# Attention and a gated feed-forward on one core: two products of the second layer split once more, with their sums on GpSimd

## The chip, the core and the metric

The kernel runs on one NeuronCore of a Trainium2 chip. Its engines run side by side, each with its own queue of instructions, and wait for one another through semaphores: TensorE (PE, matmuls; its weight loads are listed as PEld), VectorE (DVE), ScalarE (ACT), GpSimd (POOL) and SyncE (SP), which here only issues transfers. TensorE writes into PSUM[...]; VectorE and ScalarE read PSUM[...]. Everything else lives in SBUF, a memory of 128 partitions.

The metric is the device time of one execution in microseconds (us). Comparisons leave disturbed runs out.

## The reference

Linear attention without softmax, a norm per head, and a feed-forward layer with a sigmoid gate:

```python
# q, k, v: (8 batches, 8 heads, 576 positions, 64), float32
kv  = einsum('bhsd,bhse->bhde', k, v)
o   = einsum('bhsd,bhde->bhse', q, kv)
x   = o / sqrt(mean(o * o, axis=-1) + 1e-6) * g_norm       # then (4608 tokens, 512)
h   = sigmoid(x @ w_gate) * (x @ w_val)                    # (4608, 1536)
out = h @ w_out                                            # (4608, 512)
```

The weights come as 8-byte floats and are converted on the chip. All matmuls are in fp32.

## The kernel before

Tokens are worked in nine chunks of 512 (`G`). Chunk 0 is computed with plain matmuls while weights still arrive; chunks 1 to 8 each run a *first layer* (x to h) and a *second layer* (h to out), and both use a scheme of Strassen's kind: a product of two matrices, each cut into 2 x 2 blocks, takes seven block products in place of eight, and sums of blocks before and after. In the first layer some of the seven are split by seven once more. In the second layer, the blocks of h are halves of its tokens and of its 1536 columns (`NFT` = 12 tiles of 128, so `NF2` = 6), and the blocks of w_out are halves of its rows and columns (`DH` = 256). The sums of h are made by VectorE at the end of the first layer, the sums of w_out (`t2w`) once.

```python
P, G, GH = 128, 512, 256                     # GH: half a chunk; h1, h2: its two halves

def sg_tile():                               # gates, and results on their way out
    return sb.tile([P, G], FP32, tag="sg", name="sg", bufs=4)

free = deque([4, 2, 3, 0, 1])                # PSUM banks
def take():
    i = free.popleft()
    return i, bank(i)[:, 0:GH]
def give(i):
    free.append(i)

def slot():                                  # one step of other work, between matmuls
    if fill:
        fill.popleft()()

# sums of h, when one = gv[c, f] and two = gv[c, f + NF2] are done
s12[c, f] = s = hp.tile([P, G], FP32, tag="gv", name="s12")
tt(out=s[:, h1], in0=one[:, h2], in1=two[:, h2], op=ALU.add)
tt(out=s[:, h2], in0=s[:, h1], in1=one[:, h1], op=ALU.subtract)          # L854
tt(out=one[:, h2], in0=one[:, h1], in1=one[:, h2], op=ALU.subtract)
tt(out=s4[c, f], in0=two[:, h1], in1=s[:, h2], op=ALU.subtract)

def second_layer_fast(c):
    b = {(j, n): w2[:, NF2 * (j - 1):NF2 * j, DH * (n - 1):DH * n] for j in (1, 2) for n in (1, 2)}
    d1, d2 = slice(0, DH), slice(DH, DM)
    for g in range(2):
        t1, t2 = slice(P * g, P * g + P), slice(GH + P * g, GH + P * g + P)
        (i_a, pa), (i_b, pb) = (take() for _ in range(2))
        last = (c, g) == (NG - 1, 1)         # here two products are cut into halves of 128 columns
        parts = [slice(0, DH // 2), slice(DH // 2, DH)] if last else [slice(0, DH)]

        def product(ps, hs, ws, new):
            for f in range(NF2):
                nc.tensor.matmul(ps, hs(f), ws[:, f, :], start=(new and f == 0), ...)    # L870
                if f % 3 == 2:
                    slot()

        product(pa, lambda f: gv[c, f][:, t1], b[1, 1], True)
        o2 = sg_tile()
        nc.scalar.copy(out=o2[:, d1], in_=pa)
        product(pb, lambda f: s12[c, f][:, t2], t2w[2], True)
        o1 = sg_tile()
        tt(out=o1[:, d2], in0=pb, in1=o2[:, d1], op=ALU.add)
        product(pa, lambda f: gv[c, f + NF2][:, t1], b[2, 1], False)     # the one product of two added in PSUM
        nc.scalar.copy(out=o1[:, d1], in_=pa)
        if last:
            store(c, g, o1, d1)
        product(pb, lambda f: gv[c, f][:, t2], t2w[3], False)
        tt(out=o2[:, d2], in0=pb, in1=o2[:, d1], op=ALU.add)
        # ... product of s12 (t1) with t2w[1], added to o2[:, d2]
        product(pb, lambda f: gv[c, f + NF2][:, t2], t2w[4], False)
        tt(out=o2[:, d1], in0=pb, in1=o2[:, d1], op=ALU.add)
        store(c, 2 + g, o2)
        # ... product of s4 (t1) with b[2, 2], added to o1[:, d2]
        if not last:
            store(c, g, o1)
        if g == 1:
            load_late(c + 2)                 # keys and values of a later batch
```

Around it, in the order in which they are issued:

```python
def store(c, t, ot, cols=slice(0, DM), queues=(nc.sync,)):
    # ... pieces of n rows that are together in DRAM; for batches from 2 on n is 32, 64 or 96:
    queues[i % len(queues)].dma_start(
        out=rows.rearrange("(r p g i) d -> i r g p d", p=QB, g=JH, i=2)[half, r, c0 // QB:(c0 + n) // QB],
        in_=ot[r0:r0 + n, cols])             # QB = 32: g of 1, 2 or 3, p of 32

def load_late(b):                            # 9 tiles of 128 x 512 that take over tiles of h
    # ... mains[n, name] = hp.tile(..., tag="gv"), filled by nc.sync.dma_start, for k and v

def feed(b):                                 # attention for batch b, as steps for slot():
    # ... turns of q (DVE), kv_mm (PE, L354), copies (ACT), u_mm (PE, L395), squares, roots, norms,
    #     x_turn (DVE, L420) and the transfers that put x into xT

def x_sums(c):                               # the eight sums of x for the next first layer, by VectorE
    # ... four of 128x512 (L691 to L694), four of 128x128 (L701 to L704)

for c in range(1, NG):
    if c + 1 < B:
        steps = feed(c + 1)
        if c == 1:                           # the sums of w_out, in twelve pieces, on VectorE
            i = 4
            while w2_sums:
                steps.insert(i, (DVE, w2_sums.popleft()))
                i += 3
        spread(steps, ...)
    first_layer_fast(c)                      # p1 of each of its six steps: matmuls, then a sg tile
    sums_of(c + 1)                           # x_sums go to the end of the steps
    second_layer_fast(c)
    flush()                                  # what is left of the steps
```

In the first layer the sums of the weights for the next step (`tw`, L720, and `tx`, L713) are made by GpSimd, with `nc.gpsimd.tensor_tensor`.

Of the kernel before, what the change touches and what calls it, by code (L numbers as in the profile page):

```python
# [10 lines left out]
FP32 = mybir.dt.float32  # L11
# [4 lines left out]
ALU = mybir.AluOpType  # L16
# [4 lines left out]
def kernel(  # L21
# [11 lines left out]
    nc = tc.nc  # L33

    B, H, S, HD = q.shape
    T, DM = out.shape
    DF = moe_w_gate.shape[1]
    P = 128
# [22 lines left out]
    NFT = DF // P  # L61
    G = 512
    GH = G // 2
    NG = T // G
# [3 lines left out]
    sb = ctx.enter_context(tc.tile_pool(name="sb", bufs=2))  # L68
# [36 lines left out]
    def load_late(b):  # L105


        if b >= B:
            return
        mains = {}  # L110
        for n in range(NHP):
            for name, src in (("k", k), ("v", v)):
                mains[n, name] = t = hp.tile([P, G], FP32, tag="gv", name="kv")
                nc.sync.dma_start(out=t.rearrange("p (h c) -> p h c", h=2),
                                  in_=src[b, 2 * n:2 * n + 2, 0:S4].rearrange("h (p j) d -> p h (j d)", j=NK4))
        rest = hp.tile([P, G], FP32, tag="gv", name="kv")
        for i, src in enumerate((k, v)):
            for r in range(2):
                nc.sync.dma_start(out=rest[PH * r:PH * r + PH, GH * i:GH * i + GH].rearrange("p (h d) -> p h d", d=HD),
                                  in_=src[b, NHP * r:NHP * r + NHP, S4:S].rearrange("h p d -> p h d"))  # L120
        kv_late[b] = mains, rest
# [213 lines left out]
    def slot():  # L335
        if fill:
            fill.popleft()()
# [122 lines left out]
    def spread(steps, at):  # L460

        n = 0
        for engine, step in steps:
            while engine == DVE and n < 7 * NF2 and n % 7 not in at:
                fill.append(idle)
                n += 1
            fill.append(step)
            n += 1

    def flush():  # L470
        while fill:
            fill.popleft()()

    gv = {}
# [3 lines left out]
        return gv[c, f]  # L478

    def sg_tile():  # L480
        return sb.tile([P, G], FP32, tag="sg", name="sg", bufs=4)

    def store(c, t, ot, cols=slice(0, DM), queues=(nc.sync,)):

        r0 = i = 0
        while r0 < P:
            b, s = divmod(G * c + P * t + r0, S)
            rows = out[S * b:S * b + S, cols]
            if b < 2:
                j, p = divmod(s, NP)  # L490
                n = min(P - r0, NP - p)
                queues[i % len(queues)].dma_start(out=rows.rearrange("(p j) d -> j p d", j=NJ)[j, p:p + n],
                                                  in_=ot[r0:r0 + n, cols])
            else:
                half, c0 = divmod(s, S // 2)
                r, c0 = divmod(c0, XC)
                n = min(P - r0, XC - c0)
                queues[i % len(queues)].dma_start(
                    out=rows.rearrange("(r p g i) d -> i r g p d", p=QB, g=JH, i=2)[half, r, c0 // QB:(c0 + n) // QB],
                    in_=ot[r0:r0 + n, cols])  # L500
            r0 += n
            i += 1
# [7 lines left out]
    def bank(i):  # L510
        return (psum_mm if i < 2 else psum).tile([P, 512], FP32, tag=f"mm{i}", name="mm")
# [3 lines left out]
    def mm0_ps():  # L515
        return bank(next(turns0) % 2)

    def mm_ps():
        return bank((2, 3, 0, 1)[next(turns) % 4])

    def at_ps():
        return psum.tile([P, NQ, 512], FP32, tag="at", name="at")
# [4 lines left out]
# [7 lines that stand above are left out]
    def early(n):  # L534

        shared = []

        def ps(kind):
            if kind == "q":
                return shared[0]  # L540
            t = psum0.tile([P, 2, 512], FP32, tag="kq" if kind == "kv" else f"ux{n % 2}", name="two")
            if kind == "kv":
                shared.append(t)
                return t[:, :, JH * P:]
            return t
        return ps


    class Plain:
# [9 lines left out]
        def gate(self):  # L559
            self.sg = sg_tile()  # L560
            nc.scalar.activation(out=self.sg, in_=self.ps[0], func=AF.Sigmoid)
# [18 lines left out]
    a = [attention(n, early(n)) for n in range(NE)]  # L580
# [19 lines left out]
    for token in order.split():  # L600
        name = token.rstrip("0123456789.")
        n = [int(i) for i in token[len(name):].split(".")]
        f = n[0]
        if name == "b":
            if f not in blks:
                if f == 3:
                    psum_ctx.__exit__(None, None, None)
                    psum = ctx.enter_context(tc.tile_pool(name="psum", bufs=1, space=bass.MemoryType.PSUM))
                    ps = (mm_ps(), mm_ps())
                else:  # L610
                    ps = (mm0_ps() if f else warm, mm0_ps())
# [29 lines left out]
    for f in range(4, NFT):  # L641
        if f == NFT - 1:
            last = at_ps()
# [6 lines left out]
    ps = [mm_ps() for _ in range(G // P)]  # L650
# [22 lines left out]
    NF2 = NFT // 2  # L673
    DH = DM // 2
    h1, h2 = slice(0, GH), slice(GH, G)
    tt = nc.vector.tensor_tensor
    sx, tw, s12, s4 = {}, {}, {}, {}
# [171 lines left out]
    def h_sums(c, f):  # L849
# [5 lines left out]
        tt(out=one[:, h2], in0=one[:, h1], in1=one[:, h2], op=ALU.subtract)  # L855
        tt(out=s4[c, f], in0=two[:, h1], in1=s[:, h2], op=ALU.subtract)

    def second_layer_fast(c):
        b = {(j, n): w2[:, NF2 * (j - 1):NF2 * j, DH * (n - 1):DH * n] for j in (1, 2) for n in (1, 2)}
        d1, d2 = slice(0, DH), slice(DH, DM)  # L860
        for g in range(2):
            t1, t2 = slice(P * g, P * g + P), slice(GH + P * g, GH + P * g + P)
            (i_a, pa), (i_b, pb) = (take() for _ in range(2))

            last = (c, g) == (NG - 1, 1)
            parts = [slice(0, DH // 2), slice(DH // 2, DH)] if last else [slice(0, DH)]

            def product(ps, hs, ws, new):
                for f in range(NF2):
                    nc.tensor.matmul(ps, hs(f), ws[:, f, :], start=(new and f == 0), stop=(f == NF2 - 1),  # L870
                                     skip_group_check=True)
                    if f % 3 == 2:
                        slot()

            product(pa, lambda f: gv[c, f][:, t1], b[1, 1], True)
            o2 = sg_tile()
            nc.scalar.copy(out=o2[:, d1], in_=pa)
            product(pb, lambda f: s12[c, f][:, t2], t2w[2], True)
            o1 = sg_tile()
            tt(out=o1[:, d2], in0=pb, in1=o2[:, d1], op=ALU.add)  # L880
            product(pa, lambda f: gv[c, f + NF2][:, t1], b[2, 1], False)
            nc.scalar.copy(out=o1[:, d1], in_=pa)
            if last:
                store(c, g, o1, d1)
            product(pb, lambda f: gv[c, f][:, t2], t2w[3], False)
            tt(out=o2[:, d2], in0=pb, in1=o2[:, d1], op=ALU.add)
            pcs = []
            for x in parts:
                i_c, pc = take()
                pc = pc[:, 0:x.stop - x.start]  # L890
                pcs.append((i_c, pc))
                product(pc, lambda f: s12[c, f][:, t1], t2w[1][:, :, x], True)
                o2x = o2[:, DH + x.start:DH + x.stop]
                tt(out=o2x, in0=pc, in1=o2x, op=ALU.add)
            product(pb, lambda f: gv[c, f + NF2][:, t2], t2w[4], False)
            tt(out=o2[:, d1], in0=pb, in1=o2[:, d1], op=ALU.add)
            store(c, 2 + g, o2)
            give(i_a)
            give(i_b)
            for (i_c, pc), x in zip(pcs, parts):  # L900
                give(i_c)
                product(pc, lambda f: s4[c, f][:, t1], b[2, 2][:, :, x], False)
                y = slice(DH + x.start, DH + x.stop)
                tt(out=o1[:, y], in0=pc, in1=o1[:, y], op=ALU.add)
                if last:
                    store(c, g, o1, y, (nc.sync, nc.scalar))
            if not last:
                store(c, g, o1)
            if g == 1:
                load_late(c + 2)  # L910

    def sums_of(c):
        if c < NG:
            fill.append(lambda: fill.extendleft(reversed(x_sums(c))))
# [17 lines left out]
    t2w = {i: sums.tile([P, NF2, DH], FP32, name=f"t2w{i}", bufs=1) for i in (2, 3, 4)}  # L932
# [14 lines left out]
# [3 lines that stand above are left out]
            if c == 1:  # L950

                i = 4
                while w2_sums:
                    steps.insert(i, (DVE, w2_sums.popleft()))
                    i += 3
            spread(steps, (1, 2, 3, 4, 5) if c == 1 else (2, 3, 4, 5))
        first_layer_fast(c)
        sums_of(c + 1)
        second_layer_fast(c)
        flush()  # L960
# [30 lines left out]
```

## Time and profile before

| what | us |
|---|---|
| time, median of 3 runs | 1076.38 (1076.11 to 1077.92) |
| span of the profiled execution | 1073.9 |
| TensorE busy | 1062.2 |
| VectorE busy | 712.0 |
| GpSimd busy | 442.1 |
| ScalarE busy | 309.0 |
| one second layer with attention's matmuls in it (chunk 5) | 38.3 |
| one second layer without (chunk 7) | 36.3 |

A line of groups in the profile names the line of the kernel, the engine, the operation, the tiles written and read with their shapes, the count, the busy time in us and the mean of one in ns, and after the second bar the idle time of the engine just before, with what ended most of it. A line of the timeline or of the chain gives start and length in us, counted from the start of the span. Matmuls are pipelined: a record lasts longer than the distance to the next one.

### The profile page before, as it was taken

The numbers are of one execution on the slowest core, as the hardware profiler recorded it, in microseconds if no ns is written. First come the engines' busy times: TensorE is split into PE (matmuls) and PEld (weight loads), VectorE is DVE, ScalarE is ACT, GpSimd is POOL, SyncE is SP. The second block draws the span as 40 slices with busy tenths as digits, with TensorE's granted clock in tenths as the row PEclk, the third lists the DMA queues.
The fourth block names the chain that finished last, engine by engine and source line by source line (L and its number), as shares of the span: only waits on it lengthen the run. The fifth ranks groups of instructions, "written<-read, shape, count | busy, mean of one in ns | idle before, by whom it ended". The sixth has DMA issues, their size and how long they took to land.

```text
span 1073.9 us, 19464 instructions
## 1 busy us (share of the span) xinstructions
PE 1062.2 (99%) x7514; PEld 882.4 (82%) x7514; DVE 712.0 (66%) x1461; ACT 309.0 (29%) x737; POOL 442.1 (41%) x630
## 2 busy tenths in 40 slices
PE   8999999999999999999999999999999999999997
PEld 7544448888888888888888888888888888888886
DVE  4897767894579547863778357945786388628841
ACT  4654323331243113320433134312431122112210
POOL 0000035880367216640666046713663077307800
PEclk9999999999999999999999999999999999999999
DMA  9944710002400141012301140014001200010001
GB/s 259 254 157 157 244 29 22 24 17 60 119 12 13 45 128 36 12 35 62 100 23 34 42 120 13 25 45 137 13 12 27 58 2 1 2 38 1 1 1 40
DMA packets 69115, 64.96 MB, mean 60 GB/s; under 512 B 23712, under 2 KB 63008, under 8 KB 69024
## 3 DMA queue, kind: packets, MB, share of 16 engines
q1 hardware_dynamic: 68768, 63.69, 21.1%
q8 instruction: 60, 0.98, 0.4%
q14 instruction: 31, 0.25, 0.1%
q10 hardware_dynamic: 256, 0.03, 0.1%
HBM read 47.19 MB, written 9.44 MB: 53 GB/s over the span
## 4 chain that ended last, share of the span: by engine, by line
PE 97%; DVE 1%; DMA 1%; SPq 0%; issue 0%; ACT 0%; DVEq 0%
PE mm L728 46%; PE mm L870 27%; PE mm L732 7%; PE mm L556 7%; PE mm L653 4%; PE at L395 2%; PE at L354 1%; PE at L556 1%; DMA q<-in_q_dram 1%; PE two L291 0%; PE two L261 0%; PE mm L634 0%; PE two L318 0%; PE two L272 0%; PE at L360 0%; SPq L97 0%
## 5 line engine op out<-in xcount | busy, mean ns | idle before, releaser
L720 POOL TENSOR_TENSOR tw<-gv 128x256 f32<-128x256 f32 x192 | 156.2, 823 | 232.1 <-DVE w L202 145.0
L728 PE MATMUL mm<-xT,tw 128*128 128x256 f32 x768 | 198.4, 381 | 0.0
L728 PE MATMUL mm<-sx,tw 128*128 128x256 f32 x768 | 197.4, 380 | 0.0
L802 POOL TENSOR_TENSOR sg<-sg 128x256 f32<-128x256 f32 x48 | 35.6, 742 | 341.1 <-ACT sg L801 340.9
L720 POOL TENSOR_TENSOR tw<-gv,tw 128x256 f32<-128x256 f32 x192 | 155.0, 828 | 0.0
L728 PEld LDWEIGHTS mm<-xT,tw 128*128 128x128 f32 x768 | 137.3, 190 | 17.5 <-issue 2.9
L728 PEld LDWEIGHTS mm<-sx,tw 128*128 128x128 f32 x768 | 134.9, 191 | 12.4
L773 DVE TENSOR_TENSOR gv<-gv,sg 128x256 f32<-128x256 f32 x192 | 108.7, 585 | 0.0
L728 PE MATMUL mm<-sx,gv 128*128 128x256 f32 x384 | 91.2, 380 | 0.0
L728 PE MATMUL mm<-xT,gv 128*128 128x256 f32 x384 | 90.8, 379 | 0.0
L870 PE MATMUL mm<-w,gv 128*128 128x256 f32 x384 | 89.1, 381 | 0.7 <-DVE gv L773 0.7
L870 PE MATMUL mm<-t2w,gv 128*128 128x256 f32 x384 | 88.7, 381 | 0.0
L870 PE MATMUL mm<-w,s 128*128 128x256 f32 (+1 forms) x408 | 88.3, 367 | 0.0
L764 ACT ACTIVATE sg<-sg 128x256 f32<-128x256 f32 x96 | 40.0, 416 | 151.0 <-DVE sg L763 150.9
L739 ACT COPY sg<-mm 128x256 f32<-128x256 f32 x96 | 35.8, 373 | 162.7 <-PE mm L728 160.9
L870 PEld LDWEIGHTS mm<-w,gv 128*128 128x128 f32 x384 | 72.5, 190 | 12.2 <-DVE gv L773 2.5
L870 PEld LDWEIGHTS mm<-w,s 128*128 128x128 f32 x408 | 74.1, 190 | 9.4
L728 PEld LDWEIGHTS mm<-xT,gv 128*128 128x128 f32 x384 | 72.9, 190 | 10.4 <-issue 0.5
L728 PEld LDWEIGHTS mm<-sx,gv 128*128 128x128 f32 x384 | 72.5, 190 | 10.0
L870 PEld LDWEIGHTS mm<-t2w,gv 128*128 128x128 f32 x384 | 72.4, 190 | 10.0
L556 PE MATMUL mm<-xT,gv 128*128 128x512 f32 x176 | 77.4, 594 | 0.0
L745 DVE TENSOR_TENSOR gv<-mm,sg 128x256 f32<-128x256 f32 x96 | 37.0, 413 | 41.2 <-PE mm L728 37.8
(120 smaller groups left out, 1548.4 us busy)
## 6 DMA issues: line engine op xcount, KB each, us to landing
q<-in_q_dram SPq DMA_DIRECT2D x24, 288.0 KB
st<-in_moe_w_gate_dram SPq DMA_DIRECT2D x12, 512.0 KB
st<-in_moe_w_val_dram SPq DMA_DIRECT2D x12, 512.0 KB
st<-in_moe_w_out_dram SPq DMA_DIRECT2D x12, 512.0 KB
kv<-in_k_dram SPq DMA_DIRECT2D x24, 256.0 KB
kv<-in_v_dram SPq DMA_DIRECT2D x24, 256.0 KB
out_dram<-sg SPq DMA_DIRECT2D x23, 192.0 KB
xT<-xTs SPq DMA_DIRECT2D x48, 72.0 KB
```

Source lines behind the costliest of these rows:

```text
L395: nc.tensor.matmul(u[HD * e:HD * e + HD, r, o:o + HD], qTs[QB * r:QB * r + QB, (n0 + which) % 2, c:c + PH], kvq[QB * r:QB * r + QB, (n0 + ...
L556: nc.tensor.matmul(self.ps[i], w[("wg", "wv")[i], self.f][:, m, :], xT[self.c][:, m, :], start=(m == 0), stop=(m == NMT - 1), skip_group_c ...
L653: nc.tensor.matmul(ps[t], gv[0, f][:, P * t:P * t + P], w["wo", f], start=(f == 0), stop=(f == NFT - 1), skip_group_check=True)
L720: nc.gpsimd.tensor_tensor(out=tw[f, i], in0=b[in0], in1=b[in1] if isinstance(in1, tuple) else tw[f, in1], op=ALU.subtract)
L728: nc.tensor.matmul(ps, wt[:, m, :], xs[:, m, :], start=(new and m == 0), stop=(m == NK - 1), skip_group_check=True)
L732: nc.tensor.matmul(ps, wt, xs, start=new, stop=True, skip_group_check=True)
L739: nc.scalar.copy(out=d["sg"][:, h2], in_=d["pa"])
L745: tt(out=d["h"][:, h1], in0=d["pb"], in1=d["sg"][:, h2], op=ALU.add)
L764: nc.scalar.activation(out=d["sg"][:, h2], in_=d["sg"][:, h2], func=AF.Sigmoid)
L773: tt(out=d["h"][:, h], in0=d["h"][:, h], in1=d["sg"][:, h], op=ALU.mult)
L802: nc.gpsimd.tensor_tensor(out=g2[:, h1], in0=g2[:, h1], in1=g2[:, h2], op=ALU.add)
L870: nc.tensor.matmul(ps, hs(f), ws[:, f, :], start=(new and f == 0), stop=(f == NF2 - 1), skip_group_check=True)
```

## The change

The two products per token group that are taken with h's upper columns, `gv[c, f + NF2]` with `t2w[4]` and with `b[2, 1]`, are no longer computed as matmuls of 256 columns. For both token groups together each is a product of 256 tokens x 768 by 768 x 256, and is cut into 2 x 2 blocks again: seven small products of three matmuls, with 128 columns each. The purpose is less matmul work, 21 matmuls of 128 columns in place of 12 of 256.

The sums that this takes, four of h and four of the weights per product, are made by GpSimd in every chunk, 48 instructions of 128 x 128. There is no room for new tiles: they are written into halves of tiles of h (`gv`, `s12`) whose products are done. The order of the products changes for this: the same product for both token groups, one after the other, then the next. The results of all four token tiles are open at once, hence five buffers in place of four. They are stored after the first split (the second half of the tokens) and after the second (the first half). In chunk 1 the sums of w_out are put two steps apart in place of three.

```diff
-        return sb.tile([P, G], FP32, tag="sg", name="sg", bufs=4)
+        return sb.tile([P, G], FP32, tag="sg", name="sg", bufs=5)
...
+    def sums2(x, out, weights):
+        o = dict(zip((1, 2, 4, 3), out))
+        ...
+        for i, in0, in1 in ops:                      # four sums
+            for j in range(N3):                      # N3 = 3
+                u0, u1 = (x[n][j] if isinstance(n, tuple) else o[n][j] for n in (in0, in1))
+                nc.gpsimd.tensor_tensor(out=o[i][j], in0=u0, in1=u1, op=...)
+        return o
...
+        a4, a2 = h_quarters(gv, hi, 2), h_quarters(gv, hi, 0)
+        b4, b2 = w_quarters(t2w[4]), w_quarters(b[2, 1])
+        for g in pair:
+            i_, pa = take()
+            product(pa, of(gv, lo, g), b[1, 1], True)
+            o2[g] = sg_tile()
+            nc.scalar.copy(out=o2[g][:, d1], in_=pa)
+            give(i_)
+        tw4 = sums2(b4, thirds(of(gv, lo, 0) + of(gv, lo, 1)), True)
+        for g in pair:
+            i_b[g], pb[g] = take()
+            product(pb[g], of(s12, lo, 2 + g), t2w[2], True)
+            o1[g] = sg_tile()
+            nc.scalar.copy(out=o1[g][:, d1], in_=o2[g][:, d1])
+            tt(out=o1[g][:, d2], in0=pb[g], in1=o2[g][:, d1], op=ALU.add)
+        sa4 = sums2(a4, thirds(of(s12, lo, 2) + of(s12, lo, 3))[:3], False)
+        for g in pair:
+            product(pb[g], of(gv, lo, 2 + g), t2w[3], False)
+            ...
+        sa2 = sums2(a2, thirds(of(gv, lo, 2) + of(gv, lo, 3))[:3], False)
+        ...                                          # s12 with t2w[1], both groups
+        tw2_ = sums2(b2, thirds(of(s12, lo, 0) + of(s12, lo, 1)), True)
+        ...                                          # s4 with b[2, 2], both groups
+        def split(o, x, a, sa, w_, tw_, done=None):
+            (i_d, pd), (i_e, pe), (i_f, pf), (i_h, ph) = (take() for _ in range(4))
+            pd, pe, pf, ph = (ps[:, 0:P] for ps in (pd, pe, pf, ph))
+            def small(ps, hs, ws, new):
+                for j in range(N3):
+                    nc.tensor.matmul(ps, hs[j], ws[j], start=(new and j == 0), ...)
+            small(pd, a[1, 1], w_[1, 1], True)
+            add(o[0][:, l], pd)                      # VectorE, from PSUM into the result
+            small(pf, a[1, 2], w_[2, 1], True)
+            add(o[0][:, l], pf)
+            slot()
+            small(pd, sa[2], tw_[2], False)
+            add(o[0][:, r], pd)
+            small(pe, sa[1], tw_[1], True)
+            add(o[1][:, r], pe)
+            slot()
+            small(pd, sa[3], tw_[3], False)
+            ...                                      # added to both halves of o[1] at once
+            small(ph, a[2, 2], tw_[4], True)
+            add(o[1][:, l], ph)
+            slot()
+            if done:
+                done()
+            small(pe, sa[4], w_[2, 2], False)
+            add(o[0][:, r], pe)
+            slot()
+            ...
+        split(o2, d1, a4, sa4, b4, tw4)
+        for g in pair:
+            store(c, 2 + g, o2[g])
+        if ends:                                     # the last chunk
+            for g in pair:
+                store(c, g, o1[g], d2)
+            split(o1, d1, a2, sa2, b2, tw2_, lambda: [store(c, 1, o1[1], d1), store(c, 0, o1[0], tok[0])])
+            store(c, 0, o1[0], tok[1], (nc.sync, nc.scalar))
+        else:
+            split(o1, d1, a2, sa2, b2, tw2_)
+            for g in pair:
+                store(c, g, o1[g])
+        load_late(c + 2)
...
-                    i += 3
+                    i += 2
```

More of the change, by code (lines that the diff above doesn't have):

```diff
@@ L856, in h_sums @@
         tt(out=s4[c, f], in0=two[:, h1], in1=s[:, h2], op=ALU.subtract)
+    N3 = NF2 // 2
+    d1, d2 = slice(0, DH), slice(DH, DM)
+    tok = [slice(P * i, P * i + P) for i in range(G // P)]
+    def sums2(x, out, weights):
+        o = dict(zip((1, 2, 4, 3), out))
+        if weights:
+            ops = ((1, (1, 2), (1, 1)), (2, (2, 2), 1), (4, (2, 1), 2), (3, (2, 2), (1, 2)))
+        else:
+            o[3] = x[2, 1]
+            ops = ((1, (2, 1), (2, 2)), (2, 1, (1, 1)), (3, (1, 1), (2, 1)), (4, (1, 2), 2))
+        for i, in0, in1 in ops:
+            for j in range(N3):
+                u0, u1 = (x[n][j] if isinstance(n, tuple) else o[n][j] for n in (in0, in1))
+                nc.gpsimd.tensor_tensor(out=o[i][j], in0=u0, in1=u1,
+                                        op=ALU.add if i == 1 and not weights else ALU.subtract)
+        return o
@@ L858, in second_layer_fast @@
     def second_layer_fast(c):
         b = {(j, n): w2[:, NF2 * (j - 1):NF2 * j, DH * (n - 1):DH * n] for j in (1, 2) for n in (1, 2)}
[L860 to L870, printed above, removed]
-                                     skip_group_check=True)
[L872 to L910, printed above, removed]
@@ new lines, in second_layer_fast, with product, of, thirds @@
+        ends = c == NG - 1
+        pair = range(2)
+        lo, hi = range(NF2), range(NF2, NFT)
+        def product(ps, hs, ws, new):
+            for f in range(NF2):
+                nc.tensor.matmul(ps, hs[f], ws[:, f, :], start=(new and f == 0), stop=(f == NF2 - 1),
+                                 skip_group_check=True)
+                if f % N3 == N3 - 1:
+                    slot()
+        def of(tiles, fs, t):
+            return [tiles[c, f][:, tok[t]] for f in fs]
+        def thirds(tiles):
+            return [tiles[i:i + N3] for i in range(0, len(tiles), N3)]
@@ new lines, in h_quarters, with w_quarters @@
+        def h_quarters(tiles, fs, t):
+            return {(i, k): of(tiles, fs[N3 * (k - 1):N3 * k], t + i - 1) for i in (1, 2) for k in (1, 2)}
+        def w_quarters(ws):
+            return {(k, n): [ws[:, f, tok[n - 1]] for f in range(N3 * (k - 1), N3 * k)] for k in (1, 2) for n in (1, 2)}
+        a4, a2 = h_quarters(gv, hi, 2), h_quarters(gv, hi, 0)
+        b4, b2 = w_quarters(t2w[4]), w_quarters(b[2, 1])
+        o2, o1, pb, pc, i_b, i_c = {}, {}, {}, {}, {}, {}
+        for g in pair:
[4 more added lines that the diff above has]
+            give(i_)
@@ new lines, in second_layer_fast @@
+        tw4 = sums2(b4, thirds(of(gv, lo, 0) + of(gv, lo, 1)), True)
[8 more added lines that the diff above has]
+            product(pb[g], of(gv, lo, 2 + g), t2w[3], False)
+            tt(out=o2[g][:, d1], in0=pb[g], in1=o2[g][:, d1], op=ALU.add)
+            give(i_b[g])
@@ new lines, in second_layer_fast @@
+        sa2 = sums2(a2, thirds(of(gv, lo, 2) + of(gv, lo, 3))[:3], False)
+        for g in pair:
+            i_c[g], pc[g] = take()
+            product(pc[g], of(s12, lo, g), t2w[1], True)
+            tt(out=o2[g][:, d2], in0=pc[g], in1=o2[g][:, d1], op=ALU.add)
+        tw2_ = sums2(b2, thirds(of(s12, lo, 0) + of(s12, lo, 1)), True)
+        for g in pair:
+            product(pc[g], of(s4, lo, g), b[2, 2], False)
+            tt(out=o1[g][:, d2], in0=pc[g], in1=o1[g][:, d2], op=ALU.add)
+            give(i_c[g])
@@ new lines, in split, with add @@
+        def split(o, x, a, sa, w_, tw_, done=None):
+            (i_d, pd), (i_e, pe), (i_f, pf), (i_h, ph) = (take() for _ in range(4))
+            pd, pe, pf, ph = (ps[:, 0:P] for ps in (pd, pe, pf, ph))
+            l, r = slice(x.start, x.start + P), slice(x.start + P, x.stop)
+            def small(ps, hs, ws, new):
+                for j in range(N3):
+                    nc.tensor.matmul(ps, hs[j], ws[j], start=(new and j == 0), stop=(j == N3 - 1),
+                                     skip_group_check=True)
+            def add(t, ps):
+                tt(out=t, in0=ps, in1=t, op=ALU.add)
+            small(pd, a[1, 1], w_[1, 1], True)
[9 more added lines that the diff above has]
+            small(pd, sa[3], tw_[3], False)
+            y = o[1][:, x].rearrange("p (n c) -> p n c", n=2)
+            tt(out=y, in0=y, in1=pd.unsqueeze(1).to_broadcast([P, 2, P]), op=ALU.add)
+            small(ph, a[2, 2], tw_[4], True)
[5 more added lines that the diff above has]
+            add(o[0][:, r], pe)
+            slot()
+            for i in (i_d, i_f, i_h, i_e):
+                give(i)
@@ new lines, in second_layer_fast @@
+        split(o2, d1, a4, sa4, b4, tw4)
+        for g in pair:
+            store(c, 2 + g, o2[g])
+        if ends:
+            for g in pair:
+                store(c, g, o1[g], d2)
+            split(o1, d1, a2, sa2, b2, tw2_, lambda: [store(c, 1, o1[1], d1), store(c, 0, o1[0], tok[0])])
+            store(c, 0, o1[0], tok[1], (nc.sync, nc.scalar))
+        else:
+            split(o1, d1, a2, sa2, b2, tw2_)
+            for g in pair:
+                store(c, g, o1[g])
+        load_late(c + 2)
```

## The prediction

> **What bounds the kernel now.** I read the busy shares first, then the chain of work that ended last, then stretches of the timeline.
>
> ```profile
> PE 1062.2 (99%) x7514; PEld 882.4 (82%) x7514; DVE 712.0 (66%) x1461; ACT 309.0 (29%) x737; POOL 442.1 (41%) x630
> ...
> PE 97%; DVE 1%; DMA 1%; SPq 0%; issue 0%; ACT 0%; DVEq 0%
> ```
>
> TensorE is busy 99% and is 97% of the chain: the time is the sum of its records, and a new wait of TensorE adds in full. One second layer (chunk 5), from the chain in order of time (start, length, what):
>
> ```profile
> 697.04 7.92 PE mm L870 x36
> 704.96 1.73 PE at L395 x131
> 706.68 28.69 PE mm L870 x132
> 735.37 1.73 PE mm L728 x8
> ```
>
> An fp32 matmul leaves two records: these 168 are 84 matmuls, 7 products x 2 token groups x 6. I call the start of such a stage T0 (here 697.0) and the start of the next first layer T1 (735.4). The last chunk shows what 128 columns cost, because the old kernel narrows two products there:
>
> ```profile
> 1055.20 2.75 PE L870 MATMUL mm<-t2w,gv 128*128 128x256 f32 x12
> ...
> 1057.79 2.84 PE L870 MATMUL mm<-w,s 128*128 128x128 f32 x24
> ...
> 1060.47 2.75 PE L870 MATMUL mm<-t2w,gv 128*128 128x256 f32 x12
> ```
>
> Records overlap, so I count starts: (1057.79 - 1055.20)/12 = 0.216 us per record of 256 columns, (1060.47 - 1057.79)/24 = 0.112 per record of 128. The other engines, from the groups by shape:
>
> ```profile
> L713 POOL TENSOR_TENSOR tx<-gv,tx 128x128 f32<-128x128 f32 x96 | 52.8, 550 | 7.5
> L825 DVE TENSOR_TENSOR sg<-mm,sg 128x128 f32<-128x128 f32 x48 | 13.4, 279 | 0.0
> L691 DVE TENSOR_TENSOR sx<-xT 128x512 f32<-128x512 f32 x8 | 5.5, 690 | 12.4 <-DMA xT<-xTs 12.4
> ```
>
> And the place that may decide, the first layer of chunk 4 (T1 = 505.83). The transfer queue (SyncE) sends the last output tile of the second layer before it and then the keys and values; TensorE uses these at 522.03, T1 + 16.2:
>
> ```profile
> 506.36 1.14 SPq L498 DMA_DIRECT2D out_dram<-sg  x2
> 507.60 0.41 SPq L114 DMA_DIRECT2D kv<-in_k_dram  x1
> ...
> 518.25 1.27 SPq L119 DMA_DIRECT2D kv<-in_v_dram  x2
> ```
>
> ```profile
> 522.03 2.08 PE L354 MATMUL at<-kv 128*64 128x64 f32 x64
> ```
>
> By the trace's records of single packets the 2,048-byte packets of output end 2.8, 8.1, 9.8, 8.9 and 7.9 us after T1 in the five first layers that load keys and values so, and the last packet of these at 11.4, 14.5, 16.3, 15.7 and 14.4. So from the second on, they land about 6.5 us after the output has left, and up to the moment of use: there is no slack in chunk 4.
>
> [...] L854 takes 0.94 us at 699.8 beside GpSimd sums and 0.42 at 1030.8 without them. [...] For chunks from 2 on, a store of 96 rows has a slowest dimension of 3 in DRAM, one of 64 rows of 2[...]: single chains of 2,048 bytes every 80 to 84 ns, 1 to 3 at a time.
>
> **Part 1, matmuls removed.** Per chunk two products of 2 x 6 matmuls go: 12 x 2 x 0.216 = 5.18 us each. In place of each come 7 x 3 matmuls of 128 columns: 21 x 2 x 0.112 = 4.69. Saved 0.49 each, 0.98 per chunk, over 8 chunks 7.8 us, 0.7%. It is all that the change can win. The tail (part 5) ends on transfers, so I count seven chunks: **-6.8**.
>
> **Part 2, sums on GpSimd.** 4 sets x 4 sums x 3 = 48 instructions of 128x128 at 0.48 to 0.64 us (L713): some 26 us per chunk. GpSimd is free after about T0 + 4 (its last tw sum of the old trace ends at 701.3). Each set may start after the products that last read its target: T0 + 5.6, 12.5, 17.7, 22.9 with 1.73 us of attention between. At 0.52 each they end at about T0 + 12, 19, 25, 31. The first split starts after 10 products, T0 + 25.9 + 1.7 = T0 + 27.6, the second near T0 + 32.5. So GpSimd has margin of 1 us or more and is not the new bound: **0**.
>
> **Part 3, the splits' own waits.** Bank pd is reused twice per split. A small product takes 6 x 0.112 = 0.67 us; its result is complete 0.16 after, the VectorE addition takes 0.28, and one other small product lies between: 0.67 - 0.16 - 0.03 - 0.28 = 0.2 us of slack. But in chunks 1 to 6 the sums for the next chunk's x fall into these slots: the old trace has u_mm at slot 6, then 13 steps, so x sum 0 takes slot 20 and 1 to 7 take 21 to 27, which now are the splits. Each 512-wide sum (0.69 us, up to 1.1 beside GpSimd) put between pays the slack of 0.2: 0.1 to 0.6 us of wait per reuse, some 0.5 per chunk: **+3**. The wait of x sum 0 for xT (12.4 us in six chunks) should shrink, since no store now goes ahead of those transfers.
>
> **Part 4, stores bunched in front of the keys.** Before, the four tiles of a chunk left at about T0 + 18, T0 + 29, T1 - 2 and T1. Now two leave after the first split (T1 - 4.3) and two after the second (from T1 + 0.4, four transfers of 0.6 us), so keys and values start at T1 + 2.9 instead of T1 + 1.9[...]. Estimate of the end of output after chunks 2 to 5: T1 + 9.5, 12.5, 13 and 11; plus 6.4 for what follows, less the moment of use, 16.2: waits of 0, 2.7, 3.2 and 1.2 in the first layers of chunks 3 to 6: **+7**, with an uncertainty of 4.
>
> **Part 5, the tail.** Before, half the last chunk's output left at 1045.5 to 1056. Now all of it waits for the first split, T0 + 31. [...] 14 us, to about T0 + 47 with the first latency; before, the last packet was at T0 + 42.8: **+4**. Five buffers for sg cover it: four tiles are now alive at once and the next p1 needs one. The weight sums of chunk 1, packed two steps apart, only move VectorE work: **0**.
>
> Sum: -6.8 + 0 + 3 + 7 + 4 = +7. The two largest positive terms rest on a reading of the transfers that few packets support, and the saving is measured; I take 2 us off: 1076.4 + 5 = **1081 us**.
>
> **Rivals.** *Clean gain:* TensorE waits for nothing new, x sums fit[...]: 1076.4 - 6.8 + 1 = 1070.5. For it: 97% TensorE, and VectorE idles 2 us between the old products. Against: slack of 0.2 us in pd and no slack in chunk 4's keys. *VectorE or GpSimd sets the pace:* [...]sums stretch to 0.65 us, the second split waits for tw2_ and pd for late additions, 2 us in each of 8 chunks: -6.8 + 16 = 1085.5, with the tail 1089.[...] *Transfers decide,* as in parts 4 and 5: 1081.
>
> **Range and chances.** With the splits at +0.5 to +6, keys at +1 to +11 and the tail at +1 to +5, the sum runs from -4 to +15, the ends unlikely together: 1073 to 1090. 2% is 21.5 us, beyond any of these sums: faster 0.01, within 0.95, slower 0.04.
>
> **What would show it.** Right: second layers with 0.216 and 0.112 us per record and 1 us less of matmul; TensorE idle before L354 until DMA of kv in the first layers of chunks 4 to 6; waits for VectorE in the splits below 1 us per chunk; the last VectorE instruction earlier relative to T0 but the end later. Wrong: keys landing as early as before (part 4 falls, and the time is below 1076), or GpSimd named as releaser of the splits' matmuls (part 2 falls).

## The result and the profile after

The changed kernel takes 1092.54 us (median of 4 runs, 1089.27 to 1093.98), 1.0143 times the time before as a ratio of the means (95% interval 1.0118 to 1.0168): 16 us slower. The prediction was 1081 with a range of 1073 to 1090. The page of the changed kernel, busy shares and the shares of the chain by engine and by line:

```profile
span 1090.5 us, 20737 instructions
...
PE 1064.8 (98%) x7778; PEld 889.7 (82%) x7778; DVE 741.8 (68%) x1555; ACT 307.6 (28%) x737; POOL 604.0 (55%) x1014
...
PE 90%; DMA 6%; SPq 1%; POOL 1%; DVE 0%; issue 0%; ACT 0%; ACTq 0%; POOLq 0%
PE mm L728 43%; PE mm L888 19%; PE mm L556 7%; PE mm L732 7%; PE mm L947 5%; DMA out_dram<-sg 4%; PE mm L653 4%; PE at L395 2%; DMA kv<-in_v_dram 1%; PE at L354 1%; DMA v<-in_v_dram 1%; PE at L556 1%; PE two L261 0%; PE two L291 0%; POOL tw L720 0%; PE two L318 0%
```

TensorE falls from 97% to 90% of the chain and transfers rise from 1% to 6%, of them stores of the output (DMA out_dram<-sg) 4%. GpSimd is busy 162 us longer and has 1%. Now the second layer of chunk 1 in the chain: ten whole products (L888), then both splits (L947).

```profile
237.60 7.79 PE mm L888 x36
...
247.22 18.33 PE mm L888 x84
265.55 9.63 PE mm L947 x84
```

The 84 small records take 9.63 us, 0.115 each, and the profile shows no idle time of TensorE before any of them. By the first starts of TensorE's lines in the timeline a second layer of chunks 2 to 6 lasts 37.61 us where it lasted 38.34. So the matmul part brought most of its gain. The losses lie at the beginning of the first layers. ScalarE and TensorE in the first layer of chunk 3 (T1 = 389.0), each from its timeline; the bracket is the idle time before and what ended it:

```profile
393.59 0.37 ACT L739 COPY sg<-mm 128x256 f32<-128x256 f32 x1 [3.13 <-DMA out_dram<-sg]
393.86 0.27 ACT L791 COPY sg<-mm 128x128 f32<-128x128 f32 x1
...
394.18 0.30 PEld L732 LDWEIGHTS mm<-sx,tx 128*128 128x128 f32 x2 [2.36 <-ACT sg L791]
394.19 0.49 PE L732 MATMUL mm<-sx,tx 128*128 128x128 f32 x2 [1.95 <-ACT sg L791]
```

The second p1's copy (L739) wants a buffer for its gate, and the buffer is free only when a stored result has left it. The chain names the store, 7.83 us from its start to its landing, and the copy that it releases:

```profile
385.60 7.83 DMA out_dram<-sg
...
393.59 0.37 ACT sg L739
```

ScalarE's next copy (L791) stands behind L739, and TensorE needs that one: its weight loads wait 2.4 us, its matmuls 2.0. In all, L739 waits so in six first layers, 12.1 us together on ScalarE. Then TensorE's clock drops. The stretches after that wait, each with its length, the busy times (and counts) of TensorE, its weight loads, VectorE, ScalarE and GpSimd, then the granted clock, the share of the transfer engines and GB/s:

```profile
392.00:394.00 2.00, 0.23 (x2) 0.00 (x0) 0.42 (x1) 0.41 (x2) 0.00 (x0) 1.00 0.74 143
394.00:396.00 2.00, 1.81 (x8) 1.61 (x9) 0.00 (x0) 0.40 (x2) 0.00 (x0) 0.78 0.83 236
396.00:398.00 2.00, 2.00 (x7) 1.66 (x6) 0.85 (x2) 1.24 (x3) 0.72 (x1) 0.50 0.90 263
398.00:400.00 2.00, 2.00 (x10) 1.74 (x10) 1.48 (x5) 0.89 (x2) 0.73 (x1) 0.87 0.95 308
```

The record of the clock has three stretches of 3.41 us at half speed within the kernel, from 395.1, 528.2 and 647.7, each after a wait; at half speed each should cost half its length, 1.7 us (an estimate). The kernel before has none before its end. And the keys, in the place shown before, now with T1 = 506.95 (SyncE's queue, then TensorE):

```profile
502.82 7.23 SPq L498 DMA_DIRECT2D out_dram<-sg  x8
510.16 2.14 SPq L114 DMA_DIRECT2D kv<-in_k_dram  x1
...
522.83 1.27 SPq L119 DMA_DIRECT2D kv<-in_v_dram  x2
```

```profile
527.00 0.69 PE L354 MATMUL at<-kv 128*64 128x64 f32 x16 [1.37 <-DMA kv<-in_v_dram]
```

Eight stores now go in one run, and the keys follow at T1 + 3.2 where they followed at T1 + 1.9. The packets of output end 13.4 us after T1 (10.1 before, counted alike) and the last of keys and values at 20.1 (16.5 before). TensorE waits within its key products. The chain shows how the one hangs on the other:

```profile
509.50 11.17 DMA out_dram<-sg
...
520.73 6.13 DMA kv<-in_v_dram
...
527.00 0.69 PE at L354 x16
```

The load of 520.73 doesn't only land late, it is issued late: SyncE holds it back until the store of 509.50 has landed. They share no tile. In the trace the transfers of SyncE's queue use eight semaphores in turn, and this load takes the one of the store issued eight transfers before it. In the kernel before, the load in this place waited in the same way, for a store that landed 10.4 us after T1; here it is 13.7.

The 16.6 us between the two spans, from the first starts of TensorE's lines in both timelines:

| part | before | after | difference |
|---|---|---|---|
| second layers of chunks 1 to 7, sum | | | -6.1 |
| first layers, start to key products (chunks 3 to 6) | 16.4 each | 20.3, 16.8, 17.4, 18.7 | +7.7 |
| first layers of chunks 7 and 8, whole | 71.5 each | 72.0 each | +0.9 |
| key products themselves (chunks 4, 5) | 2.4 each | 4.4, 6.0 | +5.6 |
| from there to the next second layer (chunks 4, 5) | 57.65 each | 59.3, 58.9 | +3.0 |
| start of the last second layer to the end | 44.6 | 49.8 | +5.2 |

The second and third rows are waits for a gate buffer, 8.6 us, with one of the three slow stretches of the clock (chunk 3); the fourth (with the products of L360) and fifth are the keys and the other two stretches, 8.6. With 0.5 us from the part before chunk 1's second layer the differences make 16.8.

### The profile page after: what moved, and what is told of

Same layout as the page of the kernel before. It is cut to its first block, busy times and chain, and to the rows that moved or that the text cites. A ratio compares the mean times of both kernels' runs of the same rounds, so it can differ in the third digit from the quotient of the medians.

```text
span 1090.5 us, 20737 instructions
## 1 busy us (share of the span) xinstructions
PE 1064.8 (98%) x7778; PEld 889.7 (82%) x7778; DVE 741.8 (68%) x1555; ACT 307.6 (28%) x737; POOL 604.0 (55%) x1014
## 4 chain that ended last, share of the span: by engine, by line
PE 90%; DMA 6%; SPq 1%; POOL 1%; DVE 0%; issue 0%; ACT 0%; ACTq 0%; POOLq 0%
PE mm L728 43%; PE mm L888 19%; PE mm L556 7%; PE mm L732 7%; PE mm L947 5%; DMA out_dram<-sg 4%; PE mm L653 4%; PE at L395 2%; DMA kv<-in_v_dram 1%; PE at L354 1%; DMA v<-in_v_dram 1%; PE at L556 1%; PE two L261 0%; PE two L291 0%; POOL tw L720 0%; PE two L318 0%
## 5 line engine op out<-in xcount | busy, mean ns | idle before, releaser
L728 PE MATMUL mm<-sx,tw 128*128 128x256 f32 x768 | 200.6, 384 | 0.0
L739 ACT COPY sg<-mm 128x256 f32<-128x256 f32 x96 | 35.8, 373 | 273.6 <-PE mm L728 257.6
L773 DVE TENSOR_TENSOR gv<-gv,sg 128x256 f32<-128x256 f32 x192 | 110.9, 597 | 0.0
L888 PE MATMUL mm<-w,s 128*128 128x256 f32 x384 | 84.2, 379 | 0.0
L888 PEld LDWEIGHTS mm<-w,s 128*128 128x128 f32 x384 | 73.0, 190 | 9.9
L728 PEld LDWEIGHTS mm<-xT,gv 128*128 128x128 f32 x384 | 72.3, 190 | 10.0 <-issue 0.5
L556 PEld LDWEIGHTS mm<-xT,gv 128*128 128x128 f32 x176 | 32.7, 190 | 37.4 <-issue 35.9
L763 DVE TENSOR_TENSOR sg<-mm,sg 128x256 f32<-128x256 f32 x96 | 40.6, 423 | 30.8 <-PE mm L728 30.5
L749 DVE TENSOR_TENSOR gv<-mm,gv 128x256 f32<-128x256 f32 x96 | 40.3, 420 | 30.2 <-PE mm L728 28.9
L713 POOL TENSOR_TENSOR tx<-gv,tx 128x128 f32<-128x128 f32 x96 | 53.3, 555 | 7.5
```

What stands on the lines that cost most here:

```text
L556: nc.tensor.matmul(self.ps[i], w[("wg", "wv")[i], self.f][:, m, :], xT[self.c][:, m, :], start=(m == 0), stop=(m == NMT - 1), skip_group_c ...
L713: nc.gpsimd.tensor_tensor(out=tw2[i], in0=in0, in1=tw2[in1] if isinstance(in1, int) else in1, op=ALU.subtract)
L728: nc.tensor.matmul(ps, wt[:, m, :], xs[:, m, :], start=(new and m == 0), stop=(m == NK - 1), skip_group_check=True)
L749: tt(out=d["h"][:, h2], in0=ps, in1=d.pop("u")[:, h2], op=ALU.add)
L763: tt(out=d["sg"][:, h2], in0=d["pb"], in1=d["sg"][:, h2], op=ALU.add)
L773: tt(out=d["h"][:, h], in0=d["h"][:, h], in1=d["sg"][:, h], op=ALU.mult)
```

## The experiments

After the result I kept the theory of transfers from the prediction, in a wider form: the stores, bunched and with 2 or 3 packets under way at once for about half of the time or more, hold up a gate buffer and the keys. The rival was GpSimd with its sums, or the small matmuls with their many additions.

### The GpSimd sums left out

```diff
-                nc.gpsimd.tensor_tensor(out=o[i][j], in0=u0, in1=u1, op=...)
+                pass
```

> Leaves out the 48 GpSimd sums of each chunk; the splits read whatever the tiles hold, all else is as in the change (1092.5 us). Theory of transfers ([...]TensorE waits for a gate buffer and for keys): the sums cost TensorE nothing, 1090 to 1094. Rival, GpSimd (sums hold up the splits or VectorE): 1080 or less.

Measured: 1092.07 us, ratio 1.0139 (1.0121 to 1.0156). 48 instructions per chunk less on GpSimd change nothing beyond the spread of the runs. GpSimd's new sums fall as a cause.

### The split undone, the order kept

```diff
-        split(o2, d1, a4, sa4, b4, tw4)          # and the like for o1; all sums2 left out
+        for g in pair:
+            i_, ps = take()
+            product(ps, of(gv, hi, 2 + g), t2w[4], True)
+            tt(out=o2[g][:, d1], in0=ps, in1=o2[g][:, d1], op=ALU.add)
+            give(i_)
```

> Keeps the new order, the late stores and five buffers, but computes the two products whole, with 256 columns, and without GpSimd sums: the split alone is undone. Theory of transfers: the same waits stay and each second layer is 0.7 us longer, 1095 to 1100. Rival, GpSimd or the small matmuls as cause: back to the time before, 1075 to 1080.

Measured: 1081.29 us, the median of three executions (1082.70 with a fourth in it, which took 2261 us and was the profiled one, so that this run has no trace to compare), ratio 1.0056 (1.0039 to 1.0073). Both expectations missed. It is 11 us faster than the change with more matmul work, so a theory of order and stores alone doesn't hold: something in the split matters, and it isn't GpSimd.

### Seven gate buffers

```diff
-        return sb.tile([P, G], FP32, tag="sg", name="sg", bufs=5)
+        return sb.tile([P, G], FP32, tag="sg", name="sg", bufs=7)
-    t2w = {i: sums.tile([P, NF2, DH], FP32, ...) for i in (2, 3, 4)}
+    t2w = {i: sums.tile([P, NF2, DH], FP32, ...) for i in (2, 4)}
+    t2w[3] = b22                                 # its sum is left out, for room
```

> Seven sg buffers in place of five (room is made by leaving out the tile of b22 - b12, which a product reads as b22: same work for TensorE). Theory of transfers: the waits of p1's gate copy for a stored tile go, 8.6 us with the slow clock after one of them; the waits for keys stay, 1081 to 1087. Rival, the waits only move (the keys' wait grows by as much): 1089 or more.

Measured: 1088.14 us, ratio 1.0106 (1.0091 to 1.0121): 4.4 less than the change, between the two expectations. The trace has no wait for a gate buffer left, but the key products of chunks 3 to 6 now last 3.3, 4.5, 6.6 and 3.9 us in place of 2.4. TensorE's timeline in chunk 5:

```profile
638.72 0.69 PE L354 MATMUL at<-kv 128*64 128x64 f32 x16 [0.85 <-DMA kv<-in_v_dram]
...
640.21 0.69 PE L354 MATMUL at<-kv 128*64 128x64 f32 x16 [0.81 <-DMA kv<-in_v_dram]
...
641.98 1.12 PE L354 MATMUL at<-kv 128*64 128x64 f32 x16 [1.08 <-DMA kv<-in_v_dram]
```

So the buffers were too few, and about half of what more of them give is lost again (the waits for a gate buffer were 8.6 us): a first layer that doesn't wait at its start comes to its keys sooner, and they aren't there. Both waits hang on the same stores.

### Stores of 32 rows

```diff
-                n = min(P - r0, XC - c0)
+                n = min(P - r0, XC - c0, QB if c < NG - 1 else XC)      # QB = 32
```

> Cuts the stores of chunks 2 to 7 into transfers of 32 rows[...]; the last chunk is as in the change. Theory of transfers: both waits go, for a gate buffer (8.6 us) and for keys (8.5 us with what follows them), 1073 to 1079. Rival, the amount of data in one bunch and not its spread, or the longer queue of issues: keys are as late as before, 1084 or more.

Measured: 1076.34 us, ratio to the kernel before 1.0003 (0.9994 to 1.0011), as the theory said. More transfers for the same data, on SyncE's queue in the first layer of chunk 3:

```profile
384.55 3.63 SPq L498 DMA_DIRECT2D out_dram<-sg  x8
389.23 0.94 SPq L492 DMA_DIRECT2D out_dram<-sg  x2
390.27 1.80 SPq L498 DMA_DIRECT2D out_dram<-sg  x4
392.17 0.40 SPq L114 DMA_DIRECT2D kv<-in_k_dram  x1
```

The packets of output end 4.4 to 5.4 us after T1 in chunks 3 to 6 (11.4 to 15.6 in the change), the keys by T1 + 15.4, and the first layers of chunks 2 to 6 reach their key products 16.4 us after T1 again. By the records of single packets, 11 or more packets of 2,048 bytes are under way at once for over half of the time in which stores run (chunks 3 and 4), where it was 2 or 3 for about half or more in the change, and no load waits for a store to land any more: in chunk 3 the eight loads of L114 go out about 0.5 us apart, from 392.17 to 395.75. Bytes, order, buffers and splits are those of the change; only the size of each transfer, with it the number of packets at once, and the number of transfers differ. That carries the whole loss but for the end: it takes 50.4 us (44.6 in the kernel before), and this 5.7 is about what the second layers save, so that the two kernels come out equal.

### Whole products, added late: an edit that missed its aim

```diff
+            banks = [take() for g in pair]
             for g in pair:
-                i_, ps = take()
-                product(ps, of(gv, hi, t0 + g), ws, True)
+                product(banks[g][1], of(gv, hi, t0 + g), ws, True)
+            for g in pair:
                 tt(out=o[g][:, x], ...)
```

> As the run with whole products (1082.7 us), but the additions of both token tiles come after the products of both, so that two tiles are done, and stored, at the same moment, as they are after a split. Theory of transfers: what the split adds in time is that its tiles end together; so this is as slow as the change or slower by the matmul work, 1090 to 1100. Rival, the 128-column matmuls or their many short additions cost the time: still 1080 to 1085.

Measured: 1080.69 us, ratio 1.0040 (1.0028 to 1.0053). By itself this speaks for the rival, but the edit didn't do what it was for. VectorE's timeline has the two additions of one pair 2.5 us apart:

```profile
382.66 0.42 DVE L941 TENSOR_TENSOR sg<-mm,sg 128x256 f32<-128x256 f32 x1
...
385.17 0.42 DVE L941 TENSOR_TENSOR sg<-mm,sg 128x256 f32<-128x256 f32 x1 [2.09 <-PE mm L888]
```

The first addition waits for its own product alone, however late it is written. The run decides nothing.

### Whole products once more, for the trace

> The kernel with whole products once more, for its trace. Theory of transfers: each tile is stored 2.6 us after the one before it, the first of a chunk's tiles some 3 us earlier than in the change, and the waits for gate buffer and keys together are below 10 us (17 in the change). Rival: the same waits as in the change.

Measured: 1080.14 us, one run. In the first layer of chunk 3 (T1 = 390.3), SyncE begins the stores 7.1 us before T1, where the change begins them 4.1 before (here, then in the change, T1 = 389.0):

```profile
383.21 4.15 SPq L498 DMA_DIRECT2D out_dram<-sg  x4
```

```profile
384.90 2.66 SPq L498 DMA_DIRECT2D out_dram<-sg  x4
```

No first layer waits for a gate buffer; the keys cost 1.5 us in chunk 5 and 0.1 in chunk 4. Below 10 us, as expected.

### Whole products whose tiles end together

```diff
+            hs = [of(gv, hi, t0 + g) for g in pair]
+            for f in range(NF2):
+                for g in pair:
+                    nc.tensor.matmul(banks[g][1], hs[g][f], ws[:, f, :], start=(f == 0), stop=(f == NF2 - 1), ...)
```

> Whole products again, but the matmuls of the two token tiles alternate, so that both tiles end together at the end of the pair (an earlier try moved only the additions, and the first tile was still stored 2.6 us before the second). Theory of transfers: with its tiles ending together the kernel gets the waits of the change back, 1088 to 1100. Rival, the split's small matmuls and short additions cost the time in some other way: as with whole products one after the other, 1079 to 1083.

Measured: 1092.95 us, ratio 1.0156 (1.0137 to 1.0174). Without a split and without its GpSimd sums, most of the loss is back: against the kernel before, the first layers of chunks 3 to 6 lose 12.7 us (16.1 in the change, 1.7 with whole products one after the other) and the end 5.3 (5.2 and 3.3). The total equals that of the change because the saving of the split is missing. SyncE's stores in the first layer of chunk 3 (T1 = 390.5), 5.0 us ahead of it, and TensorE's wait:

```profile
385.54 2.64 SPq L498 DMA_DIRECT2D out_dram<-sg  x4
390.72 0.91 SPq L492 DMA_DIRECT2D out_dram<-sg  x2
391.73 1.27 SPq L498 DMA_DIRECT2D out_dram<-sg  x2
```

```profile
394.87 0.46 PE L732 MATMUL mm<-sx,tx 128*128 128x128 f32 x2 [1.17 <-ACT sg L791]
```

Against the whole products one after the other the matmuls and additions are the same in number and size; the first tile of each pair is stored some 2.2 us later (5.0 us before T1 in place of 7.1), and it costs some 12 us over the kernel. What the split adds to the order is this: its additions go to both tiles until the end, so neither leaves much before it. What the change loses beyond this run, some 4 us in the first layers, fits its stores' start, 0.9 us later still; no run separates it.

### Stores of 32 rows in the last chunk too, with and without the change

```diff
-                n = min(P - r0, XC - c0)
+                n = min(P - r0, XC - c0, QB)
+                if c == NG - 1:
+                    queues = (nc.sync, nc.scalar)
```

> Stores of 32 rows in all of chunks 2 to 8, and in the last chunk issued in turn on SyncE's and ScalarE's queue. Theory of transfers: the waits are gone as with 32 rows before (1076.3), and the end, 50.4 us after the last second layer starts, comes down to about 43: 1066 to 1071. Rival, the end hangs on the last addition and one store's latency: 1075 to 1077.

> The same stores in the kernel before the change, as a control: what the stores alone bring without the split. It has no waits to lose but its end, 44.6 us after the last second layer starts, of which 8 after the last matmul: 1071 to 1075. If the split saves matmul time as its second layers show (5.2 us in chunks 2 to 8), this is 3 to 6 us slower than the changed kernel with the same stores; if not, equal.

Measured: the changed kernel 1066.43 us, ratio to the kernel before 0.9904 (0.9886 to 0.9923); the kernel before with the same stores 1071.53, ratio 0.9952 (0.9935 to 0.9970). In the changed kernel the end takes 40.2 us from the start of the last second layer (50.4 with stores of 32 rows in the chunks before alone). Now 28 transfers leave on two queues in 7 us; whether the cut to 32 rows or the second queue does it, the run doesn't tell:

```profile
1055.63 6.83 SPq L500 DMA_DIRECT2D out_dram<-sg  x14
1055.64 6.91 ACTq L500 DMA_DIRECT2D out_dram<-sg  x14
```

This version beats both kernels. Next to the control, the change with its split is worth 5.1 us, as expected.

## Why the prediction was wrong

The direction and the places were partly seen, the size was not: +5 predicted, +16 measured. By its steps:

- **Part 1, matmuls (-6.8):** the second layers bring 6.1, of which 0.7 is a wait for VectorE in chunk 1 that the new order doesn't have. Right in kind; a small record took 0.115 us in place of 0.112.
- **Part 2, GpSimd (0):** right. 0.45 to 0.53 us per sum, the last ends near T0 + 25 in place of 31, and leaving all of them out changes nothing.
- **Part 3, waits in the splits (+3):** wrong in the good direction. TensorE waits for nothing there.
- **Part 4, keys (+7):** right that stores make the keys late, in chunks 4 and 5 mainly; the wait at the start of chunks 3 and 6 hid theirs, as seven buffers show. The ends of output it starts from, T1 + 9.5, 12.5, 13 and 11, were the author's estimate; measured are 11.4, 13.4, 15.6 and 12.4. The size, 8.6, came close in part by luck: some 3.4 of it is the slow clock after the waits (an estimate, half of two stretches of 3.41 us), which the prediction didn't have. And the 6.4 us from the end of output to the keys is, in the chain, a load that is issued only when a store has landed and then takes 6.1.
- **Part 5, the end (+4):** right, 5.2, though its 14 us of stores were the author's estimate; 3.3 come from the order alone (whole products one after the other), the rest with tiles that end together.
- **The step that failed is one sentence of part 5:** "Five buffers for sg cover it: four tiles are now alive at once and the next p1 needs one." p1 runs twice before the first gate is used up: the first call takes the buffer that the four results leave, the second takes that of the first stored result. Its store is issued some 6 us before that (384.9 against 391 in chunk 3), and lands later than that, at 393.4. In the kernel before, with four buffers, the two that p1 takes had been stored from T0 + 18 and T0 + 28 on, the second 10 us ahead of T1 (485.6 and 495.5, ahead of chunk 4's first layer). The waits cost 8.6 us, the slow clock after one of them included. With it the sum of the prediction, +7 less the 2 taken off, would have been +14.
- **The 2 us taken off** for doubt in the transfers had no ground in the profile, and the parts doubted were the ones that held.
- **The moment at which a tile is done** is in parts 4 and 5 only as a fact (two tiles leave after each split). The prediction doesn't separate it from the order of the products; with the order kept and the split undone the kernel is 11 us faster.
- **Luck in a rival:** that VectorE or GpSimd sets the pace came nearest by its number, 1089 with the tail, and is refuted: no matmul of the splits waits for either.

What is shown: the cut of the stores into pieces of 32 rows and the moment of completion, each by a run that changes little else. What is not: how the 4.2 us that seven buffers don't bring (8.6 less 4.4) divide between the chunks' keys, since part of them is matmuls at a slower pace (in chunk 5 two groups of 16 key matmul records took 0.69 us each, the next two 1.12); and whether, with stores of 32 rows, it is the number of packets at once or the smaller piece that lets each land sooner.

## What to carry to other kernels

When a change makes several results end together, follow each result's buffer from the issue and the landing of its store to the instruction that takes the buffer next, and count the instructions that want one before the first result can be gone, not the tiles alive. Stores of 64 and 96 rows, whose outer dimension in DRAM is 2 or 3, can be cut into stores of 32 rows, with an outer dimension of 32: in the changed kernel that was worth 16 us, for twice the issues (16 per chunk in place of 8). And where one engine is 97% of the chain, a saving of 0.7% there is only worth having if the chunk's slack in transfers (here 0 to 2 us) survives it.

## What the runs showed of the hardware

- **Stores of fewer rows.** The same bytes in stores of up to 96 rows ended 11.4 to 15.6 us after T1, with 2 or 3 packets at once for about half of the time or more; in 32-row ones 4.4 to 5.4, with 11 or more at once for over half of it. Here that was worth 16 us.
- **The clock after short waits.** In the changed kernel the clock was halved for 3.41 us from 395.1, after matmuls had waited 1.95 us (chunk 3), but not after they had waited 2.04 (chunk 6). Right after key products it was halved from 528.2, a wait of 1.37 before (chunk 4), and from 647.7, waits of 0.83, 1.04 and 0.71 before (chunk 5). Chunk 3 reached its key products 3.9 us late, chunk 6 2.3, 1.6 us less without a slow stretch.
